# Agent attention into a squared-ReLU feed-forward: keys and values in tiles of 128 tokens, and the first batch in a fixed order

## The chip, the cores and the metric

The kernel runs on one core of a Trainium2 chip. The metric is the time of one execution on the device, in microseconds (us), lower is better. The core has five engines that matter here: PE (matrix products, with PEld for the loading of weights), DVE (vector), ACT (scalar functions), POOL (GpSimd) and SP, which issues all transfers. Each runs its own instructions in order and waits for the others by semaphores.

## The reference

Four batches of 12480 tokens with 128 channels, 49 agents per batch, all float32, and then one feed-forward layer over all 49920 tokens with 2048 hidden channels:

```python
def sm(a, b):
    s = scale * (a @ b.transpose(0, 2, 1))
    s = s - s.max(-1, keepdims=True)
    e = np.exp(s)
    return e / (e.sum(-1, keepdims=True) + 1e-09)
a2k = sm(agents, k)
agent_v = a2k @ v
q2a = sm(q, agents)
x = (q2a @ agent_v).reshape(B * S, D)
h = np.maximum(x @ w_in, 0.0)
return h * h @ w_out
```

The weights w_in and w_out come in as float64 and are read on the device as pairs of 32-bit words.

## The kernel before, in words

The attention output is never formed. For each batch the kernel makes a table: the 49 agents' value rows times w_in, 49 × 2048, scaled by the softmax denominators. A token's hidden row is then its 49 weights times that table. To keep float32 accuracy with the faster float32r products, numbers are split into a high and a low half: `aw_hi` holds the table's halves (98 rows, and 30 more rows of a cross term filled by a transfer), `aw_ex` the 19 remaining cross rows, repeated at four partition offsets.

**Stage A, keys of the first batch** (L443 to L446). Thirteen tiles of 960 keys are loaded (L141), each as 8 blocks of 120 tokens. `scores` (L150) multiplies each block with the agents on PE, ACT copies the result to `s` (L158), DVE keeps a running maximum `mx` (L163). `maxima` (L166) reduces it, transposes it on PE, and broadcasts the maximum of each agent to all partitions as `mb` (L183).

**Stage B, values of the first batch** (L452 to L465). Thirteen tiles of 960 values are loaded as 120 partitions × 8 × 128 (L147). `whole_values` (L192) subtracts `mb` on DVE, takes the exponential on ACT (L196), multiplies on PE with the exponentials as weights and the values as the moving side (L200), and adds the exponentials up in `es` on POOL (L206). `whole_sums` (L208) gathers both into `x`.

**Weights.** `decoded` (L90) turns 256 columns of float64 pairs into two float32 parts: one Abs on ACT (L98), five steps on DVE (L99 to L110). For w_in POOL adds the parts (L116). For w_out ACT casts the high half (L122) and POOL makes the low half in two steps (L123, L124). There are eight pieces of each. The w_in pieces are requested behind the keys and among the values; the w_out pieces are written last in the program (L472 to L477), the last four only behind the tables.

**Tables** (L243). Two small matmuls with `quad` fold the halves (L252, L253), four matmuls with w_in (L266) make the table, ACT and DVE write its halves (L268, L270), and SP moves the cross rows (L275, L277).

**Queries** (L282) make the weights of 960 tokens: scores (L290), softmax steps, the split (L190), two groups of four transposing matmuls (L312), an ACT copy into `w` (L317), and transfers of cross rows within `w` and into `x` (L320, L322).

**Main loop** (L482). Each step k handles 480 tokens by two chunks of 128 hidden channels. `first` (L341) makes the hidden rows `h` of two steps: four matmuls with `w`, four with `x`. `hidden` (L359) takes the relu `r` and the square's high half `g_hi` on ACT, the product `gg` on DVE, and the low half `g_lo` on POOL for even and on DVE for odd steps. `second` (L384), four steps later, adds six matmuls into `o`. Sixteen steps make a block of 960 tokens; 832 steps make the whole. The next batch's keys, values and tables (`background`, L401) and the next block's queries are put among these steps.

What sets the order: the main loop's instructions are chained one behind the other on each engine by `queued` (L334), the shown line of nearly all of them being L337. Everything else, all of the first batch too, is placed by a scheduler that goes by its own estimate of times, with `tc.high_priority()` at a few places; `step` (L421) holds the background behind the first batch's last instructions on three engines.

Of the kernel before, what the change touches and what calls it, by code (L numbers as in the profile page):

```python
# [38 lines left out]
def agent_attention_relu2(ctx: ExitStack, tc: tile.TileContext, qT, kT, v, agT, w_in, w_out, outT):  # L39
# [50 lines left out]
    def decoded(dec, src):  # L90

        raw = dec.tile([P, WCH, 2], U32, name="raw", bufs=4)
        flat = raw.rearrange("p n w -> p (n w)")
# [4 lines left out]
        nc.scalar.activation(t.bitcast(F32), high.bitcast(F32), AF.Abs)  # L98
        nc.vector.tensor_scalar(  # L99
# [3 lines left out]
        nc.vector.tensor_scalar(t, t, 0x07FFFFFF, 3, op0=ALU.bitwise_and, op1=ALU.logical_shift_left)  # L103
        nc.vector.scalar_tensor_tensor(
# [4 lines left out]
        nc.vector.tensor_single_scalar(rest.bitcast(U32), t, 0xFF800000, op=ALU.bitwise_and)  # L109
        nc.vector.scalar_tensor_tensor(out=rest, in0=low, scalar=2.0**-52, in1=rest, op0=ALU.mult, op1=ALU.mult)  # L110
        return t.bitcast(F32), rest

    def load_w_in(dec, n):
        cs = slice(n * WCH, (n + 1) * WCH)
# [1 line left out]
        nc.gpsimd.tensor_add(win[:, cs], t, rest)  # L116

    def load_w_out(dec, n):
        c = slice(n * WCH // C, (n + 1) * WCH // C)
        t, rest = decoded(dec, w_out.bitcast(U32).rearrange("(c p) d -> p c d", p=P)[:, c, :])  # L120
# [1 line left out]
        nc.scalar.copy(hi, t)  # L122
        nc.gpsimd.tensor_sub(t, t, hi.bitcast(F32))  # L123
        nc.gpsimd.tensor_add(lo, t, rest)  # L124
# [413 lines left out]
```

## Time and profile before

| | |
|---|---|
| median of 3 runs | 2059.88 us (2059.42 to 2061.74) |
| the profiled execution, its own time | 2060.99 us |
| its span from first to last instruction | 2059.2 us |
| PE busy | 2029.8 us, 99% |
| ACT, DVE, POOL busy | 1782.3, 1686.1, 1279.2 us |
| granted PE clock over the span | 0.992 |

Busy time is the union of an engine's instructions; a busy PE need not be at its peak. In a row of the timeline the first number is the start in us from the span's start, the second the duration. In a row of grouped instructions the last figures are the total busy time, the mean of one in ns, and the idle time of the engine just before them with what ended it. Shapes are partitions × elements. A window's row gives each engine's busy time with the number of instructions, then the granted clock (1.00 is full), the DMA engines' mean share and GB/s.

### The profile page before, as it was taken

What the parts mean: (1) busy time and instruction counts of PE and PEld (TensorE: products, weight loads), DVE (VectorE), ACT (ScalarE), POOL (GpSimd) and SP (SyncE); (2) the same over time, 40 slices, a digit from 0 to 9 for tenths busy, and PEclk for the clock granted to TensorE, in tenths of its full rate; (3) what the DMA queues carried; (4) which work ended last, traced back from release to release, by engine and by line L of the source; (5) the groups of instructions that cost most, each with busy time, mean ns of one, the idle gap of its engine ahead of it and who ended that gap; (6) DMA issues with size and microseconds to landing.
All of it is one profiled execution on the core that took longest, in us unless ns stands there. A gap on an engine that the chain in (4) does not pass through costs nothing.

```text
span 2059.2 us, 31857 instructions
## 1 busy us (share of the span) xinstructions
PE 2029.8 (99%) x11014; PEld 1589.8 (77%) x11014; DVE 1686.1 (82%) x1842; ACT 1782.3 (87%) x2100; POOL 1279.2 (62%) x1104
## 2 busy tenths in 40 slices
PE   9799999999999999999999999999999999999999
PEld 8588777777788777777778877777777777777777
DVE  5687888888887888888887788888888888888887
ACT  3478999989888899989888899998889898989897
POOL 3555787765544587776555467877555555656555
PEclk9799999999999999999999999999999999999999
DMA  9532122121122221221112212211111111111100
GB/s 288 160 92 76 59 72 74 53 77 41 45 81 65 62 72 54 72 71 57 55 54 69 68 42 61 74 58 49 42 50 36 45 36 46 37 41 36 38 23 20
DMA packets 55604, 131.36 MB, mean 64 GB/s; under 512 B 6660, under 2 KB 34388, under 8 KB 55444
## 3 DMA queue, kind: packets, MB, share of 16 engines
q1 hardware_dynamic: 55444, 129.33, 21.0%
q8 instruction: 88, 1.44, 0.3%
q14 instruction: 72, 0.59, 0.1%
HBM read 80.97 MB, written 25.56 MB: 52 GB/s over the span
## 4 chain that ended last, share of the span: by engine, by line
PE 53%; DVE 1%; issue 0%; ACT 0%
PE o L337 33%; PE h L337 16%; PE psa L290 2%; PE psa L155 1%; PE psa L312 1%; PE psa L235 1%; PE psa L266 0%; DVE h L337 0%; DVE gg L337 0%; DVE g_lo L337 0%; DVE z L301 0%; ACT r L337 0%; DVE ob L337 0%; ACT g_hi L337 0%; DVE av L241 0%
## 5 line engine op out<-in xcount | busy, mean ns | idle before, releaser
L372 POOL TENSOR_TENSOR g_lo<-gg,g_hi 128x480 fp32r<-128x480 f32 x832 | 999.2, 1222 | 685.7 <-DVE gg L337 489.1
L337 ACT ACTIVATE r<-h 128x960 f32<-128x960 f32 x832 | 800.9, 963 | 150.0 <-PE h L337 141.9
L337 ACT ACTIVATE g_hi<-r 128x960 fp32r<-128x960 f32 x832 | 837.7, 1007 | 34.1 <-POOL e L190 0.7
L337 DVE TENSOR_TENSOR h<-r,h 128x960 f32<-128x960 f32 x416 | 482.4, 1160 | 160.2 <-ACT r L337 157.8
L337 DVE TENSOR_TENSOR gg<-r,h 128x960 f32<-128x960 f32 x416 | 477.8, 1149 | 81.9 <-ACT r L337 81.0
L337 PE MATMUL o<-g_hi,wo_hi 128*128 128x480 f32 x1664 | 543.0, 408 | 0.0
L337 DVE TENSOR_TENSOR g_lo<-h,g_hi 128x960 fp32r<-128x960 f32 x416 | 480.8, 1156 | 45.2 <-ACT g_hi L337 8.1
L337 PE MATMUL o<-g_hi,wo_lo 128*128 128x480 f32 x1664 | 498.7, 381 | 0.0
L337 PE MATMUL o<-g_lo,wo_hi 128*128 128x480 f32 x1664 | 497.7, 380 | 0.0
L337 PE MATMUL h<-w,aw_hi 128*128 128x480 f32 x1664 | 483.3, 398 | 9.7 <-DVE gg L337 8.1
L337 PEld LDWEIGHTS o<-g_hi,wo_hi 128*128 128x128 f32 x1664 | 280.8, 188 | 118.8 <-issue 70.1
L337 PEld LDWEIGHTS o<-g_hi,wo_lo 128*128 128x128 f32 x1664 | 313.4, 188 | 51.3
L337 PEld LDWEIGHTS o<-g_lo,wo_hi 128*128 128x128 f32 x1664 | 313.0, 188 | 50.9
L337 PEld LDWEIGHTS h<-w,aw_hi 128*128 128x128 f32 x1664 | 289.0, 190 | 56.9 <-DVE gg L337 17.5
L337 PE MATMUL h<-x,aw_ex 19*128 19x480 f32 x1664 | 205.4, 481 | 0.1
L337 PEld LDWEIGHTS h<-x,aw_ex 19*128 19x128 f32 x1664 | 80.5, 182 | 140.7 <-issue 139.7
L290 PEld LDWEIGHTS psa<-ag,qt 128*120 128x120 f32 x816 | 102.2, 187 | 7.8 <-issue 1.4
L337 DVE COPY ob<-o 128x480 f32<-128x480 f32 x104 | 68.3, 656 | 39.8 <-PE o L337 38.3
L290 PE MATMUL psa<-ag,qt 128*120 128x49 f32 x816 | 98.1, 264 | 0.0
L190 POOL TENSOR_TENSOR vs<-vt,vs 120x1024 fp32r<-120x1024 f32 x39 | 86.3, 2213 | 16.7 <-ACT vs L188 16.4
L155 PEld LDWEIGHTS psa<-ag,kt 128*120 128x120 f32 x624 | 74.7, 185 | 4.8 <-DVE mx L163 0.6
L155 PE MATMUL psa<-ag,kt 128*120 128x49 f32 x624 | 71.9, 262 | 0.2 <-DVE mx L163 0.2
(109 smaller groups left out, 1026.6 us busy)
## 6 DMA issues: line engine op xcount, KB each, us to landing
qt<-in_qT SPq DMA_DIRECT2D x52, 480.0 KB
out_T<-ob SPq DMA_DIRECT2D x104, 240.0 KB
kt<-in_kT SPq DMA_DIRECT2D x39, 480.0 KB
vt<-in_v SPq DMA_DIRECT2D x39, 480.0 KB
x<-w SPq DMA_DIRECT2D x416, 35.6 KB
ahead<-in_kT SPq DMA_DIRECT2D x13, 480.0 KB
ahead<-in_v SPq DMA_DIRECT2D x13, 480.0 KB
w<-w SPq DMA_DIRECT2D x104, 56.2 KB
```

Source lines behind the costliest of these rows:

```text
L155: nc.tensor.matmul(sv[:, t, :], kt[:, t * TP : (t + 1) * TP], ag[:, b, :], start=True, stop=True)
L190: last[eng] = eng.tensor_sub(out[:, :, n : n + w], x, out[:, :, :w].bitcast(F32))
L235: nc.tensor.matmul(pv[:K2, :W], e[:, t, :], vs[:, t, :], start=(t == 0), stop=(t == NT - 1))
L290: nc.tensor.matmul(sv[:, t, :], qt[:, t * TP : (t + 1) * TP], ag[:, b, :], start=True, stop=True)
L312: nc.tensor.matmul(pt[:K2, t * TP : (t + 1) * TP], pp[:, j * (NT // 2) + t, :], identr, start=True, stop=True)
L337: ins = issue(*args, **kw)
L372: nc.gpsimd.tensor_sub(lo[:, n, :], gg[:, n, :], hi[:, n, :].bitcast(F32))
```

## The change

*Tiles.* The 12480 tokens of a batch are cut into 12 blocks of 8 × 128 tokens and a last one of 2 × 96, instead of 13 of 8 × 120. The host lays the keys out to match. Queries keep their 120.

*Order.* `queued` moves to the top, and wrappers `pe`, `act`, `dve`, `pool` and `sync` chain every instruction of the first batch behind the one written before it on its engine, so that this stage runs as written. It is written so: a w_in piece is requested behind each key tile and decoded between the scores; the query tile's scores lie between the transposition and the broadcast of the maxima; the w_out pieces are requested among the values; one is decoded in each of eight iterations of the values loop, ahead of the tables. The exponentials of a block are taken two iterations ahead, their subtraction in turn on POOL and DVE. `behind`, which holds the background, now names four engines.

*Products turned round.* `whole_values` takes the values as weights and the exponentials as moving side, so the result is already transposed; `quad` is not needed for the first batch, and the sum of exponentials is reduced twice into two halves.

```diff
+    blocks = [(i * KB, P, NT) for i in range(N // KB)] + [(N // KB * KB, N % KB // 2, 2)]
+    class Ordered:
+        def __getattr__(self, name):
+            issue = getattr(self.eng, name)
+            if not alone[0]:
+                return issue
+            return lambda *args, **kw: queued(issue, self.eng, *args, **kw)
+    pe, act, dve, pool, sync = (Ordered(e) for e in (nc.tensor, nc.scalar, nc.vector, nc.gpsimd, nc.sync))
...
-        vt = pool.tile([TP, NT, C], F32, name=name)
-        src = v[b, i * BLK : (i + 1) * BLK, :].rearrange("(p t) c -> p t c", p=TP)
-        last[nc.sync] = nc.sync.dma_start(vt, src)
+        at, rows, nt = blocks[i]
+        vt = pool.tile([P, KB], F32, name=name).rearrange("p (t c) -> p t c", c=C)
+        src = v[b, at : at + rows * nt, :].rearrange("(p t) c -> p t c", p=rows)
+        sync.dma_start(vt[:rows, :nt, :], src)
...
+    def whole_exps(b, i, eng):
+        _, rows, nt = blocks[i]
+        e = state[b]["s"][i][:rows, :nt, :]
+        less_maximum(b, i, e, eng)
+        act.activation(e, e, AF.Exp, scale=scale)
     def whole_values(b, i, vt):
-            nc.tensor.matmul(
-                st["pv"][:NA, :C], e[:, t, :], vt[:, t, :], start=(i == 0 and t == 0), stop=(i == NB - 1 and t == NT - 1)
+            pe.matmul(
+                st["pv"][:C, :NA], vt[:rows, t, :], e[:, t, :],
+                start=(i == 0 and t == 0), stop=(i == NK - 1 and t == nt - 1),
             )
...
-        for i in range(NB):
-            kt = load_keys(0, i, pre, "ahead")
-            run(scores(0, i, kt))
-        for n in range(WIN):
-            load_w_in(dec, n)
+        early = {i: i - 3 for i in range(3, 8)} | {9: 5, 11: 6}
+        for i in range(NK):
+            kts.append(load_keys(0, i, pre, "ahead"))
+            if 1 <= i <= NW:
+                raws[i - 1] = ask_w_in(dec, i - 1)
+            if i == NK - 3:
+                q0 = queries(0)
+                next(q0)
+            run(scores(0, i, kts[i]))
+            if i in early:
+                make_w_in(dec, early[i], raws.pop(early[i]))
+        top = maxima(0)
+        next(top)
+        next(top)
+        next(q0)
+        run(top)
+        for i in range(NK):
+            if i == NW:
+                make_w_in(dec, NW - 1, raws.pop(NW - 1))
+            vts.append(load_values(0, i, pre, "ahead"))
+            if 1 <= i <= NW:
+                raws[NW + i - 1] = ask_w_out(dec, i - 1)
+        for i in range(2):
+            whole_exps(0, i, (pool, dve)[i % 2])
+        for i in range(NK):
+            if i + 2 < NK:
+                whole_exps(0, i + 2, (pool, dve)[i % 2])
+            whole_values(0, i, vts[i])
+            next(q0, None)
+            if 3 <= i < NW + 3:
+                make_w_out(dec, i - 3, raws.pop(NW + i - 3))
         run(q0)
-    for n in range(NW):
-        with ExitStack() as es:
-            for ins in made if n >= EARLY else ():
-                es.enter_context(tc.issue_after(ins))
-            load_w_out(dec, n)
+        whole_sums(0)
+        run(tables(0))
+    behind = [chain[eng] for eng in (nc.sync, nc.scalar, nc.vector, nc.gpsimd)]
```

The built order shows three places. First ACT in the values stage, where `t<-raw` is the Abs that opens the decoding of a piece, `wo_hi<-t` its cast and `s<-s` the exponential of a block. Before:

```order
L196 ACTIVATE s_271<-s_271 120x392
L196 ACTIVATE s_285<-s_285 120x392
L98 ACTIVATE t_366<-raw_364 128x256
L196 ACTIVATE s_299<-s_299 120x392
L196 ACTIVATE s_313<-s_313 120x392
L188 CAST pp_530<-e_453 120x8x49
L98 ACTIVATE t_379<-raw_377 128x256
L98 ACTIVATE t_392<-raw_390 128x256
L98 ACTIVATE t_405<-raw_403 128x256
L317 CAST w0_560<-h_555 98x480
L98 ACTIVATE t_697<-raw_695 128x256
L98 ACTIVATE t_710<-raw_708 128x256
```

And in the change, in the middle of the values loop:

```order
L58 ACTIVATE s_293<-s_293 128x392
L58 CAST w0_573<-h_568 98x480
L58 ACTIVATE t_576<-raw_424 128x256
L58 CAST wo_hi_108<-t_576 128x256
L58 ACTIVATE s_318<-s_318 128x392
L58 ACTIVATE t_603<-raw_428 128x256
L58 CAST wo_hi_108<-t_603 128x256
L58 ACTIVATE s_332<-s_332 128x392
L58 CAST w1_630<-h_625 98x480
L58 ACTIVATE t_633<-raw_432 128x256
```

Before, exponentials came in a row and pieces were decoded two at a time behind them; now each exponential has one piece's Abs and cast behind it.

POOL in the same stage; `t<-t,wo_hi` and `wo_lo<-t,rest` finish a piece of w_out, `s<-s,mb` is a subtraction, and `mx` now holds the sum that `es` held. Before:

```order
L206 TENSOR_TENSOR es_478<-es_478,s_285 120x392
L116 TENSOR_TENSOR win_110<-t_405,rest_410 128x256
L206 TENSOR_TENSOR es_478<-es_478,s_299 120x392
L206 TENSOR_TENSOR es_478<-es_478,s_313 120x392
L123 TENSOR_TENSOR t_697<-t_697,wo_hi_111 128x256
L124 TENSOR_TENSOR wo_lo_112<-t_697,rest_702 128x256
```

In the change:

```order
L58 TENSOR_TENSOR t_576<-t_576,wo_hi_108 128x256
L58 TENSOR_TENSOR wo_lo_109<-t_576,rest_581 128x256
L58 TENSOR_TENSOR s_318<-s_318,mb_410 128x392
L58 TENSOR_TENSOR mx_146<-mx_146,s_268 128x392
L58 TENSOR_TENSOR t_603<-t_603,wo_hi_108 128x256
L58 TENSOR_TENSOR wo_lo_109<-t_603,rest_608 128x256
L58 TENSOR_TENSOR mx_146<-mx_146,s_293 128x392
```

The subtractions of every second block have moved to POOL, each behind the piece decoded before it, and the pieces of w_out stand ahead of the last sums.

PE at the first change of the token block, where `psa<-identr,pp` are the transposing matmuls of the second query tile and `h<-w` the first matmuls of two steps. Before, the w of the second tile (number 1016 there) is not yet used in these rows:

```order
L337 MATMUL h_1073<-w1_595,aw_hi_652 128x480 x2
L312 MATMUL psa_1011<-identr_94,pp_956 98x120 x4
L337 MATMUL h_1074<-w1_595,aw_hi_652 128x480 x2
L337 MATMUL h_1073<-x1_596,aw_ex_653 128x480 x2
L337 MATMUL h_1074<-x1_596,aw_ex_653 128x480 x2
L337 MATMUL o_920<-g_hi_972,wo_hi_111 128x480 x2
L337 MATMUL o_920<-g_hi_972,wo_lo_112 128x480 x2
L337 MATMUL o_920<-g_lo_974,wo_hi_111 128x480 x2
L337 MATMUL o_920<-g_hi_992,wo_hi_111 128x480 x2
L337 MATMUL o_920<-g_hi_992,wo_lo_112 128x480 x2
L337 MATMUL o_920<-g_lo_994,wo_hi_111 128x480 x2
L312 MATMUL psa_1065<-identr_94,pp_956 98x120 x4
```

In the change, where the w of the second tile is w0_999:

```order
L58 MATMUL o_1132<-g_lo_1095,wo_hi_108 128x480 x2
L183 MATMUL psa_985<-ag_82,kt_923 128x49 x8
L356 MATMUL psa_994<-identr_91,pp_939 98x120 x4
L356 MATMUL psa_1048<-identr_91,pp_939 98x120 x4
L58 MATMUL h_1209<-w0_999,aw_hi_738 128x480 x2
L58 MATMUL h_1210<-w0_999,aw_hi_738 128x480 x2
L183 MATMUL psa_1099<-ag_82,kt_983 128x49 x8
L58 MATMUL h_1209<-x0_1000,aw_ex_739 128x480 x2
L58 MATMUL h_1210<-x0_1000,aw_ex_739 128x480 x2
```

Both groups of transposing matmuls have moved to right ahead of the first matmul that uses their result. L58 in these rows is the line of `queued` in the changed kernel.

More of the change, by code (lines that the diff above doesn't have):

```diff
@@ L80, in agent_attention_relu2 @@
         )
-    split = [const.tile([TP, NT, 2 * (C + 1)], F32R, name=f"vs{i}") for i in range(2)]
+    split = [const.tile([P, NT, 2 * (C + 1)], F32R, name=f"vs{i}") for i in range(2)]
     for vs in split:
@@ L185, in halves, with less_maximum @@
+        dve.tensor_copy(st["mb"], pb[:, :NA])
     def halves(out, x, n, eng):
         w = x.shape[2]
-        nc.scalar.copy(out[:, :, :w], x)
+        act.copy(out[:, :, :w], x)
         yield
-        last[eng] = eng.tensor_sub(out[:, :, n : n + w], x, out[:, :, :w].bitcast(F32))
+        eng.tensor_sub(out[:, :, n : n + w], x, out[:, :, :w].bitcast(F32))
+    def less_maximum(b, i, out, eng):
+        st = state[b]
+        _, rows, nt = blocks[i]
+        mb = st["mb"][:rows, :].rearrange("p (o a) -> p o a", o=1).broadcast_to([rows, nt, NA])
+        eng.tensor_sub(out, st["s"][i][:rows, :nt, :], mb)
@@ L215, in whole_sums @@
-        pz = bank()
-        nc.tensor.matmul(pz[:NA, :1], e1, ones[:TP, :1], start=True, stop=True)
-        nc.vector.tensor_copy(x[:NA, C:], pz[:NA, :1])
-    def values(b, i, vt, eng):
+        e1 = small.tile([P, 2, NA], F32, name="e1")
+        for n in range(2):
+            dve.reduce_sum(e1[:, n, :], st["mx"].rearrange("p t a -> p a t"), axis=AX.X)
+        pz = bank()
+        pe.matmul(pz[:K2, :1], e1.rearrange("p h a -> p (h a)"), ones[:, :1], start=True, stop=True)
+        rl = st["rl"] = small.tile([K2, 1], F32, name="rl")
@@ L220, in values @@
+        dve.tensor_scalar_add(rl, pz[:K2, :1], 1e-9)
+        dve.reciprocal(rl, rl)
+        av = st["avT"] = small.tile([C, K2], F32, name="avT")
+        act.copy(av[:, :NA], st["pv"][:C, :NA])
+        dve.tensor_copy(av[:, NA:], st["pv"][:C, :NA])
+    def values(b, i, vt):
         st = state[b]
-        s = st["s"][i]
-        mb = st["mb"].rearrange("p (o a) -> p o a", o=1).broadcast_to([TP, NT, NA])
-        d = small.tile([TP, NT, NA], F32, name="d", bufs=2)
-        eng.tensor_sub(d, s, mb)
+        _, rows, nt = blocks[i]
+        d = small.tile([P, NT, NA], F32, name="d", bufs=2)[:rows, :nt, :]
+        less_maximum(b, i, d, pool)
@@ L232, in values @@
         yield
         pv = bank()
-        for t in range(NT):
-            nc.tensor.matmul(pv[:K2, :W], e[:, t, :], vs[:, t, :], start=(t == 0), stop=(t == NT - 1))
+        for t in range(nt):
+            pe.matmul(pv[:K2, :W], e[:, t, :], vs[:rows, t, :], start=(t == 0), stop=(t == nt - 1))
         yield
@@ L450, in agent_attention_relu2 @@
         next(q0)
[L451 to L452 removed]
+        run(top)
+        for i in range(NK):
+            if i == NW:
+                make_w_in(dec, NW - 1, raws.pop(NW - 1))
             vts.append(load_values(0, i, pre, "ahead"))
[L454 to L460 removed]
+            if 1 <= i <= NW:
+                raws[NW + i - 1] = ask_w_out(dec, i - 1)
```

258 lines of the change are left out of this document (121 added, 137 removed).

## The prediction

> **What bounds the kernel now.** I read the page first, then the busy time by windows, then the timeline of the first 140 us for the anchors, and the groups of instructions for durations.
>
> ```profile
> 8.00:20.00 12.00, 12.00 (x117) 12.00 (x117) 3.94 (x7) 3.40 (x7) 0.00 (x0) 1.00 1.03 407
> 35.10:64.90 29.80, 21.54 (x171) 20.77 (x172) 19.28 (x34) 8.47 (x18) 17.85 (x18) 0.84 1.00 247
> 83.70:105.00 21.30, 17.70 (x71) 12.71 (x71) 19.60 (x27) 15.77 (x23) 13.21 (x11) 0.68 0.42 108
> 160.00:2059.20 1899.20, 1890.16 (x10110) 1470.53 (x10108) 1574.69 (x1661) 1698.34 (x1973) 1206.80 (x1021) 1.00 0.18 54
> ```
>
> The columns of a window are its length, the busy time of PE, PEld, DVE, ACT and POOL, the clock, the DMA share and GB/s. From 160 us on PE is busy for 1890 of 1899 us at full clock: the main loop is bound by PE, and only less PE work or an earlier start moves the end. Before that lie two weak stretches: the values stage (35 to 65 us, loads at 247 GB/s, share 1.00) and the first 21 us of the main loop (clock 0.68). So the question is when PE gets a steady main loop. The anchors are these:
>
> ```profile
> 72.78 1.88 PE L155 MATMUL psa<-ag,kt 128*120 128x49 f32 x16
> ...
> 77.44 5.11 PE L266 MATMUL h<-win,avT 128*98 128x512 f32 x8 [0.76 <-ACT avT L256]
> ...
> 83.68 0.74 PEld L337 LDWEIGHTS h<-w,aw_hi 128*128 128x128 f32 x4 [1.98 <-DVE aw_lo L270]
> ```
>
> The second batch's first scores run at 72.8, the table of the first batch starts at 77.4, the main loop at 83.7.
>
> **The change, part by part.** *Keys.* Keys, query tile and the eight w_in pieces now interleave: 9.0 MB, of which all but the first 0.5 MB come after the first score at 407 GB/s, 21 us, so the last tile is scored near 29.7, against 28.7 now. Behind it DVE has a decode (2 us), a maximum and a reduction, so the transposition of the maxima comes near 33.4. Then the query tile's scores stand on PE between it and the broadcast:
>
> ```profile
> 28.54 1.84 PE L290 MATMUL h<-ag,qt 128*120 128x49 f32 x16
> ...
> 30.43 0.80 DVE L169 TENSOR_REDUCE m<-mx 120x49 f32<-120x392 f32 x1
> ...
> 93.83 3.44 PE L290 MATMUL psa<-ag,qt 128*120 128x49 f32 x16
> ```
>
> They cost 1.84 us at full and 3.44 at half clock; PE has just idled 3.7 us, so I take the latter. With 0.9 for the broadcast and its copy, mb is ready at 37.7 (36.1 to 38).
>
> *Values stage: a chain instead of a load.* One iteration that decodes a piece of w_out I call a round; there are eight. The reader finds the order of ACT and POOL in the section on the change. In it ACT takes a piece's Abs only after the exponential of the block two ahead, which waits for that block's subtraction, on POOL in one iteration and on DVE in the next, itself behind the preceding round's decoding. Behind that exponential on ACT stand Abs and the cast, and for them wait DVE's five steps and POOL's two.
>
> ```profile
> L224 POOL TENSOR_TENSOR d<-s,mb 120x392 f32<-120x392 f32 x39 | 37.2, 961 | 0.0
> ...
> L196 ACT ACTIVATE s<-s 120x392 f32<-120x392 f32 x13 | 6.5, 528 | 5.5 <-DVE s L195 5.5
> ...
> L98 ACT ACTIVATE t<-raw 128x256 f32<-128x256 f32 x16 | 6.7, 434 | 23.1 <-DMA raw<-in_w_out 10.8 <-DMA raw<-in_w_in 7.3 <-POOL es L206 2.5
> ...
> L99 DVE TENSOR_SCALAR t<-t 128x256 f32<-128x256 f32 x16 | 10.0, 628 | 10.7 <-ACT t L98 9.9 <-POOL win L116 0.9
> ...
> L103 DVE TENSOR_SCALAR t<-t 128x256 uint32<-128x256 uint32 x16 | 5.5, 351 | 0.2
> ...
> L104 DVE SCALAR_TENSOR_TENSOR t<-raw,t 128x256 uint32<-128x256 uint32 x16 | 7.5, 476 | 0.1
> ...
> L109 DVE TENSOR_SCALAR rest<-t 128x256 uint32<-128x256 uint32 x16 | 6.5, 403 | 0.3
> ...
> L110 DVE SCALAR_TENSOR_TENSOR rest<-raw,rest 128x256 f32<-128x256 uint32 x16 | 9.9, 617 | 0.2
> ...
> L195 DVE TENSOR_TENSOR s<-s,mb 120x392 f32<-120x392 f32 x13 | 9.6, 808 | 0.0
> ...
> L122 ACT CAST wo_hi<-t 128x256 fp32r<-128x256 f32 x8 | 3.2, 405 | 7.4 <-DVE t L104 7.4
> ...
> L123 POOL TENSOR_TENSOR t<-t,wo_hi 128x256 f32<-128x256 f32 x8 | 6.9, 862 | 10.3 <-ACT wo_hi L122 10.0 <-DVE rest L109 0.3
> ...
> L124 POOL TENSOR_TENSOR wo_lo<-t,rest 128x256 fp32r<-128x256 f32 x8 | 6.1, 764 | 0.7 <-DVE rest L110 0.4
> ...
> L206 POOL TENSOR_TENSOR es<-es,s 120x392 f32<-120x392 f32 x11 | 12.1, 1097 | 0.5
> ```
>
> A POOL round runs 0.96 (subtraction) + 0.53 + 0.43 + 1.46 (three DVE steps) + 1.02 (two more) = 4.40; the DVE round behind it 0.81 + 0.53 + 0.43 + 1.46 + 0.41 + 0.86 + 0.76 = 5.26. With some ten handovers of 0.04 a pair takes 9.7 to 10.1; I take 4.9 a round, 39.2 in all. These means contain waits of DVE for POOL:
>
> ```profile
> 48.27 0.95 POOL L190 TENSOR_TENSOR pp<-e,pp 120x392 fp32r<-120x392 f32 x1 [1.83 <-ACT pp L188]
> ...
> 48.42 1.08 DVE L110 SCALAR_TENSOR_TENSOR rest<-raw,rest 128x256 f32<-128x256 uint32 x1
> ...
> 52.58 0.42 DVE L110 SCALAR_TENSOR_TENSOR rest<-raw,rest 128x256 f32<-128x256 uint32 x1
> ```
>
> The same step took 1.08 us beside a POOL instruction and 0.42 alone. So 0.42 of L110's mean 0.617 is its own work. With every DVE step at that share, 0.68, of its mean, the pair loses 0.32 × (2 × 1.46 + 1.02 + 0.81) = 1.5: a round of 4.2, 33.6 in all, is the lower bound. [...]
>
> Ahead of the first round, after mb: the last w_in decode (2.0), then on POOL its addition (0.76), three subtractions and the query product (0.96 each) and two sums (1.10), then a cast (0.5): 9.3, with handovers 9.7. Behind the last: two sums (1.1 and a short 0.3), now two reductions of 0.8, one matmul and the small steps to the table (1.1): 4.1. Turning the products round and dropping the matmuls with quad lies on PE, which in this stage waits for the exponentials; if that cover went, 13 blocks of 16 passes of 0.115 would be 24 us, still less than the rounds.
>
> The table thus starts at 37.7 + 9.7 + 39.2 + 4.1 = 90.7 instead of 77.4: **+13.3** (+7 to +15).
>
> Where the loads go: with 128 partitions I expect 400 GB/s, so values and w_out (8.5 MB) are there near 50; at 247 they would be near 64. The last block is used near 83, so neither counts; if the chain were not there, the loads would cost up to 14. On SP the requests for w_out move ahead of the second batch's first keys and values, and those go behind the tables' copies. The batch's first scores stand behind the first o's in PE's order, so their landing may cost one 1.8 us wait, which the range below holds.
>
> *Start of the main loop.* The instruction counts of 83.6 to 105 and a clean stretch:
>
> ```profile
> L337 PE MATMUL h<-w,aw_hi 128*128 128x480 f32 x12 | 5.2, 545 | 4.7 <-DVE gg L337 3.2 <-DVE aw_lo L270 1.2 <-PE psa L290 0.3
> ...
> L337 PE MATMUL o<-g_hi,wo_hi 128*128 128x480 f32 x4 | 2.2, 643 | 0.0
> ...
> L155 PE MATMUL psa<-ag,kt 128*120 128x49 f32 x19 | 2.3, 267 | 0.0
> ...
> 1600.77 1.04 PE L337 MATMUL h<-w,aw_hi 128*128 128x480 f32 x4
> ...
> 1602.17 0.70 PE L337 MATMUL o<-g_hi,wo_hi 128*128 128x480 f32 x2
> ...
> 1604.89 1.04 PE L337 MATMUL h<-w,aw_hi 128*128 128x480 f32 x4
> ```
>
> Cleanly, four h with their x take 1.40 us, twelve o 2.72. So these 21.3 us did 3 × 1.40 + 2.72 + 35 score passes of 0.115 (1.84 / 16) = 10.9, lost 10.4, and had 1.9 in hand (72.78): net 8.5. Part of that is DVE decoding w_out there, which the change takes away. What stays is the filling of the pipeline:
>
> ```profile
> L337 ACT ACTIVATE r<-h 128x960 f32<-128x960 f32 x832 | 800.9, 963 | 150.0 <-PE h L337 141.9
> ...
> L337 ACT ACTIVATE g_hi<-r 128x960 fp32r<-128x960 f32 x832 | 837.7, 1007 | 34.1 <-POOL e L190 0.7
> ```
>
> The third pair of h waits for buffers that four ACT steps (3.94) and a DVE step free, so the first o comes about 9 us after the first h with 4.2 us of work done; 1 more for a clock near 0.5: 6 lost. **−2.5** (−4.5 to 0).
>
> *First change of the token block.* The built order puts both transpositions of the second query tile right ahead of the first matmul that needs them; now they stand 14.5 us ahead:
>
> ```profile
> 69.38 0.84 SPq L320 DMA_DIRECT2D w<-w  x1
> ...
> 70.27 2.88 SPq L322 DMA_DIRECT2D x<-w  x4
> ...
> 80.99 0.86 SPq L275 DMA_DIRECT2D aw_hi<-aw_lo  x1
> ...
> 117.32 0.48 PE L312 MATMUL psa<-identr,pp 120*98 120x120 f32 x4
> ...
> 131.87 0.60 PE L337 MATMUL h<-w,aw_hi 128*128 128x480 f32 x2
> ```
>
> A cast (as L196, 0.5) behind a relu or square in ACT's queue (1.0, the row of r above), issues of 0.84 + 2.88, and a landing of 1.8 (81.85 to 83.68) make 7.0 us. Behind the waiting matmul stand the next scores, 1.8, and with the first h, 0.9, that is all that PE can do meanwhile. With 1 for the wait ahead of the transpositions, for POOL's half of pp: **+5** (+2 to +8).
>
> *Batches 2 to 4.* Six of 104 value matmuls a batch go:
>
> ```profile
> L235 PE MATMUL psa<-vs,e 120*98 120x258 f32 x312 | 43.8, 283 | 0.0
> ```
>
> 18 × 43.8 / 312 = **−2.5**. Score passes become fewer (36 in three batches) but their weights wider, 128 columns for 120. No row has that form, so the saving lies between 0, if a pass grows with its columns, and 36 × 0.115 = 4 if it does not; I take 0, since the weights' bytes stay the same, and keep the 4 in the range. The reordered keys and the removed quad cost no measured time.
>
> Sum: 13.3 − 2.5 + 5 − 2.5 = +13.3 on the profiled execution's 2060.99, 2074.3; its time is 1.1 above the median, so 2073.
>
> **The rivals.** *Load-bound* (faster): the values stage is set by its loads, now and after. For it: share 1.00 at 247 GB/s. 7.4 MB at 407 would take 18.1 instead of 29.8. It decides if a round takes under its block's load, 0.8 MB or 2 us. Then −11.7 − 2.5 − 2.5 + 5: 2048. Against it: no chain of the rows above gets under 4.2. [...]
>
> *POOL's pace* (near 2060): ACT and DVE run far enough ahead that only POOL's work counts, 0.48 + 1.10 + 1.63 = 3.2 a round. −13.6 from the sum: 2059, or 2056 with a block change at 2.
>
> *Unblocked:* rounds of 4.2, block change at 2: 2073 − 5.6 − 3 = 2064.
>
> *Worse:* half clock until 115 and a block change of 8: 2080.
>
> **How the numbers follow.** Forecast 2073: 0.60. Load-bound 0.08, POOL's pace 0.12, unblocked 0.10, worse 0.10. The range 2058 to 2084 leaves out load-bound and half of POOL's pace. About 0.2%, 4 us, is what a measurement can tell. Faster: 0.08 + half of 0.12 = 0.14; same: 0.06 and a fifth of unblocked, 0.08; slower 0.78.
>
> **What would show it.** Right: table matmul near 91, wo_hi casts 4 to 5 us apart, loads over near 50 at about 400 GB/s, a PE gap of 5 us at the first block change, full PE from there. Wrong: casts 2 to 3 us apart, a table before 78, or no gap.

## The result: 28 us slower, and the profile after

The kernel after takes 2089.24 us (median of 4 runs, 2088.95 to 2089.47), the kernel before 2060.79 (4 runs, 2059.42 to 2061.74): a ratio of 1.0138, 95% interval 1.0121 to 1.0156. The profiled execution took 2089.47 us with a span of 2087.6, against 2060.99 and 2059.2. The forecast of 2073 had the direction and less than half of the size (12 us of 28); 2089 lies outside its range of 2058 to 2084.

The first view is the busy time by windows (columns as before: length, busy time of PE, PEld, DVE, ACT, POOL, clock, DMA share, GB/s). A window's count of instructions includes those under way at its edges.

```profile
4.09:7.50 3.41, 3.41 (x33) 3.41 (x32) 0.00 (x0) 0.00 (x0) 0.00 (x0) 1.00 0.98 360
7.50:10.91 3.41, 3.41 (x33) 3.41 (x32) 1.12 (x2) 0.97 (x2) 0.00 (x0) 1.00 1.00 370
10.91:14.33 3.42, 3.42 (x19) 3.42 (x17) 0.57 (x2) 0.48 (x1) 0.00 (x0) 0.50 1.03 405
35.10:64.90 29.80, 21.77 (x104) 21.39 (x103) 14.46 (x36) 7.21 (x17) 11.15 (x13) 0.50 0.46 163
...
83.70:105.00 21.30, 15.98 (x73) 15.34 (x72) 10.69 (x26) 5.75 (x15) 13.84 (x17) 0.50 0.04 13
160.00:2087.00 1927.00, 1913.00 (x10255) 1498.51 (x10255) 1593.24 (x1686) 1713.51 (x2000) 1210.70 (x1032) 1.00 0.18 55
```

The clock column is the news. PE's clock falls to half at 10.9 us and comes back at 113.3 (and is at half once more from 120.1 to 127.0). It falls while PE is busy for all of every window (3.41 of 3.41 us in the two ahead of 10.9): no pause of PE stands ahead of it. In the kernel before the clock was full in the scores and in most of the values stage; a stretch of its scores, then a step of its values stage at half clock and the one behind it:

```profile
12.10:15.51 3.41, 3.41 (x35) 3.41 (x34) 1.12 (x2) 1.02 (x3) 0.00 (x0) 1.00 1.03 406
36.00:39.41 3.41, 3.41 (x18) 3.33 (x17) 3.41 (x3) 1.59 (x4) 3.25 (x3) 0.50 0.98 252
39.41:42.83 3.42, 3.42 (x34) 3.42 (x33) 3.42 (x5) 1.34 (x3) 2.53 (x3) 1.00 0.99 243
```

The timeline of the kernel after:

```profile
35.77 7.67 PE L58 MATMUL h<-ag,ahead 128*128 128x49 f32 x36
...
51.03 0.21 DVE L58 COPY mb<-h 128x49 f32<-128x49 f32 x1 [3.14 <-PE h L58]
...
68.47 0.40 ACT L58 CAST wo_hi<-t 128x256 fp32r<-128x256 f32 x1 [1.97 <-DVE t L58]
...
77.03 0.56 ACT L58 CAST w<-h 98x480 fp32r<-98x480 f32 x1 [6.23 <-PE h L58]
...
79.14 0.41 ACT L58 CAST wo_hi<-t 128x256 fp32r<-128x256 f32 x1 [1.22 <-DVE t L58]
...
108.76 5.92 PE L58 MATMUL h<-win,avT 128*98 128x512 f32 x8 [0.56 <-DVE avT L58]
```

Each float32 matmul of a block appears as two passes on PE, 16 for a block of eight. At half clock a score pass takes 0.213 us (7.67 / 36), so the last keys are scored near 43 instead of 29.7, and mb comes at 51.2 instead of 37.7. The eight casts of wo_hi come at 62.6, 68.5, 79.1, 84.3, 88.6, 93.8, 98.0 and 102.5. Six of the seven gaps average 4.9; one is 10.7. In that one ACT waits 6.23 us for PE: the query tile's transposition stands in PE's order behind value products that run at half speed, and in ACT's order its cast stands ahead of the next piece's magnitude. The first table matmul comes at 108.76 instead of 77.44.

The first change of the token block, in the timeline:

```profile
126.93 0.43 SPq L329 DMA_DIRECT2D qt<-in_qT  x1
...
146.61 1.78 PE L334 MATMUL psa<-ag,qt 128*120 128x49 f32 x16
...
161.21 0.89 PE L356 MATMUL psa<-identr,pp 120*98 120x120 f32 x4 [1.51 <-DVE mx L192]
...
162.75 0.92 PE L356 MATMUL psa<-identr,pp 120*98 120x120 f32 x4 [0.65 <-ACT w L361]
...
165.00 1.97 PE L58 MATMUL h<-w,aw_hi 128*128 128x480 f32 x4 [1.34 <-DMA w<-w]
...
172.10 0.76 PE L58 MATMUL h<-x,aw_ex 19*128 19x480 f32 x1 [0.77 <-DMA x<-w]
172.79 0.50 PEld L58 LDWEIGHTS o<-g_hi,wo_hi 128*128 128x128 f32 x2 [0.41 <-issue]
```

The second query tile is asked for at 126.9, behind the copies of the tables. The transpositions come at 161.2, the matmuls that need them wait for the copies of w and x, and the clock is at half again from 161.1 to 178.2. All that PE waited for between 144 and 182 us (total, times, longest):

```profile
PE psa L356 <- DVE mx L192: 1.5, 1, 1.5
PE h L58 <- DMA w<-w: 1.3, 1, 1.3
PE h L58 <- DMA x<-w: 0.8, 1, 0.8
PE psa L356 <- ACT w L361: 0.6, 1, 0.6
```

To see what each stretch costs, I count the o matmuls in the trace (six to a step) and compare when a step's first one begins:

| step | before | after | difference |
|---|---|---|---|
| (first table matmul) | 77.4 | 108.8 | +31.3 |
| 0 | 100.4 | 124.9 | +24.6 |
| 10 | 129.1 | 155.1 | +26.0 |
| 18 | 152.3 | 192.8 | +40.4 |
| 208 | 610.2 | 649.7 | +39.5 |
| 416 | 1112.0 | 1148.2 | +36.2 |
| 624 | 1606.3 | 1638.6 | +32.4 |
| 831 | 2053.7 | 2081.9 | +28.2 |

So: +31.3 up to the table, −5.3 in the main loop's start, +14.4 at the block change, and −12.2 over the rest: 0.9 up to step 208, then 3.3, 3.8 and 4.2 a batch, the last batch included, in which no other batch's attention runs. The forecast had +13.3, −2.5, +5 and −2.5.

### The profile page after: what moved, and what is told of

It is laid out like the page before. It is cut to its first block, busy times and chain, and to the rows that moved or that the text cites. A ratio compares the mean times of both kernels' runs of the same rounds, so it can differ in the third digit from the quotient of the medians.

```text
span 2087.6 us, 31676 instructions
## 1 busy us (share of the span) xinstructions
PE 2051.5 (98%) x10932; PEld 1621.5 (78%) x10932; DVE 1672.7 (80%) x1835; ACT 1775.2 (85%) x2100; POOL 1275.1 (61%) x1110
## 5 line engine op out<-in xcount | busy, mean ns | idle before, releaser
L58 ACT ACTIVATE r<-h 128x960 f32<-128x960 f32 x832 | 800.7, 962 | 145.5 <-PE h L58 132.7
L58 ACT ACTIVATE g_hi<-r 128x960 fp32r<-128x960 f32 x832 | 837.5, 1007 | 34.8 <-PE o L58 1.0
L58 DVE TENSOR_TENSOR h<-r,h 128x960 f32<-128x960 f32 x416 | 482.5, 1160 | 156.7 <-ACT r L58 151.6
L58 DVE TENSOR_TENSOR gg<-r,h 128x960 f32<-128x960 f32 x416 | 478.0, 1149 | 85.4 <-ACT r L58 79.9
L58 PE MATMUL o<-g_hi,wo_hi 128*128 128x480 f32 x1664 | 539.2, 405 | 0.0
L58 DVE TENSOR_TENSOR g_lo<-h,g_hi 128x960 fp32r<-128x960 f32 x416 | 481.0, 1156 | 48.3 <-ACT g_hi L58 7.7
L58 PE MATMUL h<-w,aw_hi 128*128 128x480 f32 x1664 | 485.4, 398 | 10.7 <-DVE gg L58 7.7
L58 PE MATMUL o<-g_hi,wo_lo 128*128 128x480 f32 x1664 | 495.4, 379 | 0.0
L58 PE MATMUL o<-g_lo,wo_hi 128*128 128x480 f32 x1664 | 494.7, 378 | 0.0
L58 PEld LDWEIGHTS o<-g_hi,wo_hi 128*128 128x128 f32 x1664 | 280.9, 188 | 117.4 <-issue 69.5
L58 PEld LDWEIGHTS o<-g_hi,wo_lo 128*128 128x128 f32 x1664 | 313.3, 188 | 47.2
L58 PEld LDWEIGHTS o<-g_lo,wo_hi 128*128 128x128 f32 x1664 | 313.3, 188 | 46.7
L58 PEld LDWEIGHTS h<-w,aw_hi 128*128 128x128 f32 x1664 | 289.3, 190 | 59.3 <-DVE gg L58 20.3
L58 PE MATMUL h<-x,aw_ex 19*128 19x480 f32 x1664 | 207.9, 481 | 1.3 <-DMA x<-w 1.0
L58 PEld LDWEIGHTS h<-x,aw_ex 19*128 19x128 f32 x1664 | 81.6, 182 | 142.4 <-issue 138.1
L58 DVE COPY ob<-o 128x480 f32<-128x480 f32 x104 | 68.2, 656 | 35.9 <-PE o L58 35.5
L219 POOL TENSOR_TENSOR vs<-vt,vs 128x1024 fp32r<-128x1024 f32 (+1 forms) x39 | 81.6, 2094 | 12.6 <-ACT vs L217 12.3
L183 PEld LDWEIGHTS psa<-ag,kt 128*128 128x128 f32 (+1 forms) x588 | 76.4, 195 | 3.6
L183 PE MATMUL psa<-ag,kt 128*128 128x49 f32 (+1 forms) x588 | 72.7, 271 | 0.0
```

Source lines behind the costliest of these rows:

```text
L58: ins = issue(*args, **kw)
L183: pe.matmul(sv[:, t, :], kt[:, t * rows : (t + 1) * rows], ag[:, b, :], start=True, stop=True)
L219: eng.tensor_sub(out[:, :, n : n + w], x, out[:, :, :w].bitcast(F32))
```

## Experiments: the clock

Theory: the granted clock follows how many columns PE streams, not whether it is busy. A pass takes 0.11 us at full clock behind 128 × 128 weights whether it streams 49 columns or 128 (the kernel after, up to 10.9 us: 0.112 in the median from one begin to the next, for 43 passes of 49 and for 31 of 128). Rival: the fixed order sets the pace, and the clock only follows it. Behind each time stands its ratio to the kernel before, measured beside it, with a 95% interval. `...` marks lines left out.

**64 columns.** Edit, in scores and in products alike:

```diff
-            pe.matmul(sv[:, t, :], kt[:, t * rows : (t + 1) * rows], ag[:, b, :], start=True, stop=True)
+            pe.matmul(sw[:, t, :], kt[:, t * rows : (t + 1) * rows], cols, start=True, stop=True)
...
```

> The kernel after, but the first batch's scores and value products stream 64 columns in each pass instead of 49 (the 15 more are neighbours' columns and their results are not read); PE's passes there take 0.111 us at full clock whether they stream 49 or 128 columns, so the work costs no more. Clock theory (PE's clock is granted by how much of PE's time goes into streaming columns; 49 columns behind weights of 128 x 128 are too few to hold it or to get it back): the clock stays at 1.00 from 4 us through the scores, mb is ready near 37 instead of 51, the long round of 10.7 us is gone, the first table matmul comes near 91 instead of 108.8, and the time is 2070 to 2074. Order theory (the interleaved loads and the fixed order set the pace and the clock only follows): 2087 to 2091 and half clock as now.

Measured: 2075.63, ratio 1.0082 (1.0065 to 1.0099). The windows of a score step and of a product step:

```profile
13.80:17.20 3.40, 3.40 (x33) 3.40 (x32) 2.07 (x6) 1.44 (x4) 0.00 (x0) 1.00 1.05 405
...
47.90:51.30 3.40, 3.40 (x18) 3.40 (x17) 1.73 (x5) 1.60 (x4) 1.79 (x3) 0.50 0.44 154
```

Fifteen unused columns a pass hold the clock through the scores (full until 30.9), and mb comes at 39.2. But in PE's pause around mb the clock falls, and 64 columns do not get it back: the 10.7 us round stays, the table comes at 96.7. Half of the theory's forecast, then. At half clock 16 passes begin in 3.41 us, 994 columns here; at full clock, from 13.8 to 17.2, it was 31 passes, 1984 columns.

**Products turned back**, exponentials as weights, values streamed (128 columns):

```diff
-                st["pv"][:C, :NA], vt[:rows, t, :], e[:, t, :],
+                st["pv"][:NA, :C], e[:, t, :], vt[:rows, t, :],
...
```

> The kernel after, but the first batch's value products are turned back: exponentials as weights (49 columns wide), values streamed, 128 columns a pass, with the matmuls by quad at the end. Clock theory: half clock through the scores as now (mb at 51), but granted in full a few us after the products begin, near 60 to 63, so that the query tile's transposition no longer waits behind half-speed products: the 10.7 us round falls to 5, the table comes near 102, time 2081 to 2084. Order theory: no change, 2088 to 2092.

```profile
56.70:60.10 3.40, 3.40 (x18) 3.23 (x17) 2.04 (x4) 1.75 (x5) 2.99 (x4) 0.50 0.36 145
60.10:63.50 3.40, 3.40 (x33) 3.40 (x32) 1.74 (x5) 1.47 (x4) 1.78 (x3) 1.00 0.60 183
```

The clock returns behind the first window filled with 128-column passes, the casts are 4.8 apart, and the table comes at 102.1, all as forecast. Yet the time was 2092.32, ratio 1.0157 (1.0142 to 1.0172): the main loop had become slower. That is taken up below.

**Tiles of 120 tokens** in the kernel after, order and turn kept:

```diff
-KB = P * NT
+KB = BLK
...
-    blocks = [(i * KB, P, NT) for i in range(N // KB)] + [(N // KB * KB, N % KB // 2, 2)]
+    blocks = [(i * KB, TP, NT) for i in range(N // KB)]
...
```

> The kernel after, but keys and values in tiles of 120 tokens again (13 blocks of 960), order and turned products kept. Clock theory: full clock through the scores, since a pass of 49 columns behind 120-wide weights takes 0.105 and held the clock in the kernel before; mb near 38. The products (49 columns, weights of 120 x 128) then start behind a pause of PE: if the clock is not granted again, 208 passes of 0.213 make 44 us and the table comes near 98, time 2080 to 2084 with the 18 value matmuls of batches 2 to 4 back; if it is, 2074 to 2077. The values' loads should fall to about 250 GB/s and last until 65. Order theory: clock falls near 11 us as now, 2090 to 2094.

```profile
11.25:14.70 3.45, 3.41 (x32) 3.28 (x31) 1.45 (x4) 1.30 (x3) 0.00 (x0) 1.00 1.04 410
14.70:18.10 3.40, 3.40 (x19) 3.40 (x18) 3.19 (x9) 0.82 (x2) 0.72 (x1) 0.50 1.03 398
```

Measured: 2085.53, ratio 1.0125 (1.011 to 1.014). The clock fell here too, at 14.7, which the theory had not forecast. In the 3.41 us ahead of that only 30 passes began, where the kernel before had 32 or 33: the pieces of w_in between the keys (0.26 MB to each 0.49 MB, at 400 GB/s 1.9 us a tile against 1.67 of passes) make PE wait; two passes begin 0.21 and 0.31 us behind the one before, where the others take 0.105. So the wider weights (31 passes in the kernel after, with no such gap) and the interleaved loads each bring the number of passes in a step under that of the kernel before. The time lies outside the ranges of both theories. With the table at 106.4, 120 tokens take 2.0 us more from step 18 to step 831 than the kernel after (1891.2 and 1889.1).

**The turn alone**, in the kernel before:

```diff
-                st["pv"][:NA, :C], e[:, t, :], vt[:, t, :], start=(i == 0 and t == 0), stop=(i == NB - 1 and t == NT - 1)
+                st["pv"][:C, :NA], vt[:, t, :], e[:, t, :], start=(i == 0 and t == 0), stop=(i == NB - 1 and t == NT - 1)
...
```

> The kernel before with the first batch's value products turned round and the matmuls by quad dropped for it, nothing else changed. Clock theory: the clock falls in PE's pause ahead of the products (32.6) as before, but is not granted again at 39.4; the products run at 0.213 us a pass, 44 us from 35, so that they end near 80 to 82 instead of 72, the table comes near 86 instead of 77.4, and the time is 2066 to 2071. Order theory: the turn does nothing but save the matmuls by quad, 2058 to 2061.

```profile
35.20:65.90 30.70, 30.70 (x147) 30.70 (x146) 22.67 (x34) 7.80 (x18) 17.91 (x18) 0.50 0.99 252
...
90.09 5.22 PE L269 MATMUL h<-win,avT 128*98 128x512 f32 x8
```

Measured: 2073.24, ratio 1.0064 (1.0049 to 1.0079). PE is busy for all of 30.7 us at half clock; the table comes at 90.1 instead of 77.4. One swap of operands, with fewer matmuls behind it, costs 13 us. The order theory's 2058 to 2061 is out; the clock theory had the course right (0.50 in this window, 0.84 in the kernel before from 35.1 to 64.9) and 2 to 7 us too little (2066 to 2071, table near 86).

**128 columns** in scores and turned products of the kernel after:

```diff
+        w = 128 if alone[0] else NA
...
+        cols = ag.rearrange("c b a -> c (b a)")[:, b * NA : b * NA + w]
...
+            w = min(128, (nt - t) * NA)
...
```

> The kernel after, but the first batch's scores and turned products stream 128 columns in each pass instead of 49 (79 of them neighbours' columns whose results are not read; the last two or three passes of a block's products stream fewer). Clock theory: full clock through the scores as with 64 columns, and now granted again within two of its 3.4 us steps after the products begin, so that the round of 10.7 us goes too: mb near 39, casts of wo_hi 4.8 apart, table near 90, time 2067 to 2071. Weight theory (weights of 128 x 128 keep the clock down whatever is streamed behind them): as with 64 columns, 2074 to 2077.

```profile
36.79 0.21 DVE L58 COPY mb<-h 128x49 f32<-128x49 f32 x1 [2.15 <-PE h L58]
...
58.55 0.41 ACT L58 CAST wo_hi<-t 128x256 fp32r<-128x256 f32 x1 [1.22 <-DVE t L58]
63.70 0.41 ACT L58 CAST wo_hi<-t 128x256 fp32r<-128x256 f32 x1 [1.22 <-DVE t L58]
...
88.18 6.13 PE L58 MATMUL h<-win,avT 128*98 128x512 f32 x8 [0.56 <-DVE avT L58]
```

Measured: 2070.94, ratio 1.0051 (1.0036 to 1.0067), as the clock theory said; the weight theory is out. With its clock the values stage is what the prediction had summed up: mb at 37.0, rounds of 4.8, table at 88.2. The clock falls here too in PE's pause around mb, and comes back behind the first step filled with such passes:

```profile
41.95:45.36 3.41, 3.41 (x18) 3.41 (x18) 1.89 (x4) 1.90 (x4) 3.00 (x5) 0.50 1.04 395
45.36:48.80 3.44, 3.44 (x32) 3.44 (x32) 1.61 (x6) 1.79 (x4) 1.83 (x2) 1.00 0.73 267
```

## Experiments: the late query tile

```diff
+        asked = chain[nc.sync]
         run(tables(0))
-    behind = [chain[eng] for eng in (nc.sync, nc.scalar, nc.vector, nc.gpsimd)]
+    behind = [asked] + [chain[eng] for eng in (nc.scalar, nc.vector, nc.gpsimd)]
```

> The kernel after, but the second batch's loads (first keys, first values, next query tile) may be asked for right behind the first batch's loads instead of behind the copies of the tables; PE's order at the first change of the token block then has the transpositions some 8 steps earlier. Load theory (the stall of some 15 us between the tenth and the fourteenth step comes from the query tile that arrives too late): first o within 3 us of 125, but the loss at the block change falls under 3 us, time 2073 to 2079. Chain theory (the steps from the query scores to the transposed weights are too long whenever they start): 2087 to 2091.

```profile
91.95 0.43 SPq L329 DMA_DIRECT2D qt<-in_qT  x1
...
123.41 3.44 PE L334 MATMUL psa<-ag,qt 128*120 128x49 f32 x16
...
145.76 0.48 PE L356 MATMUL psa<-identr,pp 120*98 120x120 f32 x4
```

Measured: 2075.04, ratio 1.0065 (1.0047 to 1.0083). The tile is asked for 35 us earlier, and the transpositions stand 15 us earlier than they did. Steps 10 and 14 begin 11.7 us apart instead of 26.0, and the clock stays full through the change (its mean over the span is 0.972, against 0.969 in the kernel after). The first o came at 129.2, 4.3 us later than in the kernel after, which the load theory had not forecast (within 3). The chain theory is out: no wait of PE is left at the change, though 22 us lie between the tile's scores and its transpositions, against 14.6 in the kernel after. No engine of the kernel after waits for the query tile itself; its scores stand late in PE's order, at 146.6, and the edit moves them in the built order as well as the load. So what cost the 14 us is the tile's late request together with the late place of its steps; the two were not separated.

## Experiments: the pitch of the main loop

Two clean steps take 4.12 us in the kernel before (shown in the prediction) and 4.08 after:

```profile
1619.24 1.04 PE L58 MATMUL h<-w,aw_hi 128*128 128x480 f32 x4
...
1623.32 1.02 PE L58 MATMUL h<-w,aw_hi 128*128 128x480 f32 x4
```

The instructions are the same. In the kernel with the products turned back they take 4.13 again (h at 1653.17 and 1657.30). What differs there is only the size of small tiles ahead of the main loop's: everything behind lies 192 bytes a partition lower in SBUF. So I moved it back, and moved the kernel before's tiles up by 160 (a tile of 40):

```diff
+    small.tile([P, 48], F32, name="gap")
     aw = ctx.enter_context(tc.tile_pool(name="aw", bufs=2))
```

> The kernel of e2_unturned with an unused tile of 192 bytes a partition ahead of the main loop's tiles, so that the tables, the query tiles and everything of the main loop lie at the same places in SBUF as in the kernel after (in e2_unturned they lay 192 bytes lower). Address theory (where these tiles lie sets the pitch of the main loop's passes): a step of the last batch falls from 2.156 us to 2.137 as in the kernel after, and the time from 2092.3 to 2080 to 2082, the first o staying near 118.7. Work theory (the slower steps of e2_unturned come from what it does or from the chip, not from addresses): 2091 to 2094.

> The kernel before with an unused tile of 160 bytes a partition ahead of the main loop's tiles, nothing else. Address theory, with a pattern that repeats within 1024 bytes (the tables and main loop tiles then lie as in the kernel after, modulo 1024): a step of the last batch falls from 2.157 to 2.137 us, and the time to 2044 to 2050. Address theory with a longer pattern: anything between 2044 and 2062. Work theory: 2058 to 2062.

The two kernels' h of successive pairs of steps:

```profile
1644.96 1.04 PE L58 MATMUL h<-w,aw_hi 128*128 128x480 f32 x4
1649.03 1.03 PE L58 MATMUL h<-w,aw_hi 128*128 128x480 f32 x4
```

```profile
1615.59 1.04 PE L338 MATMUL h<-w,aw_hi 128*128 128x480 f32 x4
1619.66 1.04 PE L338 MATMUL h<-w,aw_hi 128*128 128x480 f32 x4
```

Both take 4.07. The first measured 2081.53, ratio 1.0102 (1.0087 to 1.0117), 10.8 less than without its gap. The second measured 2048.74, ratio 0.9943 (0.9927 to 0.9958): an unused tile of 160 bytes makes the kernel before 12.9 us faster. From step 18 to step 831 the kernel before took 1901.4 us, with the unused tile 1888.9, and the kernel after 1889.1: the tile alone accounts for the whole −12.2 of the table above. The kernel after has the better pitch though nothing in the diff aims at it. Why these addresses are better, and of which tile, was not tried.

## Experiments: the decoding, and both repairs

**Both repairs** (128 columns, loads first):

> The kernel after with both repairs, 128 columns a pass (e6_wide128) and the second batch's loads ahead of the tables' copies (e7_loads_first), the decoding left in the values stage. If the two costs are separate they add up: 2089.2 - 18.3 - 14.2 = 2056.7, 2054 to 2060. If a faster start brings another wait ahead of the first block change, 2062 or more.

The edits are the two shown above. Measured: 2053.03, ratio 0.9955 (0.994 to 0.9969), 1 us under the forecast range: together the repairs give 36.2 us, 3.7 more than the two apart (18.3 and 14.2), and the repaired change is faster than the kernel before. It is not faster than the kernel before with the gap, whose interval overlaps its own.

**Decoding moved behind the table.** The first two tries also cut the buffers of encoded pieces to four, and that held up other loads:

```diff
-            if 3 <= i < NW + 3:
-                make_w_out(dec, i - 3, raws.pop(NW + i - 3))
...
+            make_w_out(dec, n, raws.pop(NW + n) if NW + n in raws else ask_w_out(dec, n))
```

> The kernel of e6_wide128 (128 columns a pass in scores and turned products), with the decoding of w_out taken out of the values stage: the first four pieces may be decoded at any time, the last four behind the table's steps, in the scheduler's order as in the kernel before. Chain theory (eight rounds of 4.8 us, the decoding's chain, set the values stage): without them a block costs what POOL (0.95 every second block and 1.0 for the sum) or PE (1.8) needs, 13 blocks near 24 us from 41; the first table matmul comes near 68 to 72 instead of 88. The decoding then lies beside the first steps of the main loop and costs there 6 to 10 of the 18 gained: 2059 to 2065. Load theory (the values come no faster than the rounds): table at 85 or later, 2070 or more.

> The kernel of e9_decode_behind, with the second batch's loads allowed ahead of the tables' copies as in e7_loads_first. If the three costs (clock, rounds, late query tile) are separate, this takes another 12 to 14 us off e9_decode_behind: 2046 to 2052, faster than the kernel before and about the same as the kernel before with the gap. If the decoding in the main loop's start and the earlier loads collide, 2055 or more.

Measured: 2063.03, ratio 1.0008 (0.9998 to 1.0017), and 2063.71, ratio 1.0012 (1.0003 to 1.0021). In both, keys waited behind w_in's pieces for a buffer (mb at 47.8 and 45.9), in the second PE also stood 6.84 us for the second batch's keys ahead of the table. Neither answers the question. The third try gave the late pieces buffers of their own, and again fewer to the rest (9 instead of 11 for keys and values, 6 instead of 8 for encoded pieces). Its control, with the decoding left in the rounds, has only the first edit:

```diff
-    behind = [asked] + [chain[eng] for eng in (nc.scalar, nc.vector, nc.gpsimd)]
+    behind = [asked] + [chain[eng] for eng in (nc.tensor, nc.scalar, nc.vector, nc.gpsimd)]
...
+    late = ctx.enter_context(tc.tile_pool(name="late", bufs=2))
...
+            make_w_out(late, n, w_outs[n] if n < 4 else ask_w_out(late, n))
...
```

> The kernel of e14_scores_late (both repairs, the second batch's first scores behind the table's matmuls on PE) with the whole decoding of w_out behind the table's steps, its first four pieces in buffers of their own, so that neither the keys nor the second batch's loads wait for a buffer of it as they did in e9_decode_behind and e10_behind_loads. Chain theory (the decoding is what makes the values stage 39 us long, and DVE and POOL have room for it later): mb near 37, products over by 64 to 68, table 68 to 74, time 2038 to 2044. Give-back theory (in the main loop's start the decoding costs what it cost between the products, since DVE and POOL are wanted there too): table as early, but the fourth step's o no earlier than in e14_scores_late, 2049 to 2054.

> The kernel of e11_wide_loads, with the second batch's first scores held behind the table's matmuls on PE, since in e12_halves_apart PE stood 5.5 us for their keys in the middle of the products. If that wait lay on the path: 2 to 4 us less than e11_wide_loads, 2049 to 2051; if it was covered by the rounds: 2052 to 2054. Control for e13_decode_late.

The timeline and two windows of the third try:

```profile
69.02 3.76 PE L58 MATMUL h<-win,avT 128*98 128x512 f32 x8 [0.56 <-DVE avT L58]
80.54 1.94 PE L58 MATMUL h<-w,aw_hi 128*128 128x480 f32 x4 [1.60 <-DMA aw_hi<-aw_lo]
```

```profile
44.00:64.00 20.00, 20.00 (x167) 20.00 (x168) 5.70 (x7) 7.11 (x16) 18.17 (x19) 0.91 0.29 94
80.54:115.70 35.16, 31.65 (x134) 23.78 (x135) 33.26 (x57) 24.01 (x37) 25.26 (x24) 0.65 0.43 142
```

Measured: 2051.70, ratio 0.9958 (0.9943 to 0.9972); the control 2053.09, ratio 0.9968 (0.9955 to 0.9981). The table comes 19 us earlier than the control's 88.0, the first o 8 us earlier, step 8 begins 1 us later, step 18 is 2.5 us ahead. In the values stage PE is then the limit: it is busy for all of the 20 us, in one stretch up to the sums, with POOL close behind (18.2 of 20). In the main loop's start DVE is busy for 33.3 of 35.2 us and PE's clock is 0.65. The time is that of the give-back theory; its sign came later than it said, since the fourth step's o was still 6.4 us earlier (113.5 against 119.9) and the gain was gone by step 8. So moving the decoding behind the table won nothing that can be measured (1.4 us, overlapping intervals); what the fewer buffers cost in it was not separated. The control beside both repairs (2053.09 and 2053.03) shows that PE's wait for the second batch's keys was covered.

**Rounds without the chain**: each piece's cast and POOL steps one iteration later, on top of both repairs.

```diff
+            if half:
+                make_w_out(i - 4, *half.pop())
             if 3 <= i < NW + 3:
-                make_w_out(dec, i - 3, raws.pop(NW + i - 3))
+                half.append(decoded(dec, raws.pop(NW + i - 3)))
...
```

> The kernel of e11_wide_loads, with each piece of w_out decoded in two halves: the magnitude and DVE's five steps in one iteration of the values loop, ACT's cast and POOL's two steps in the next, so that no engine waits there for the one before it; the same instructions otherwise. Chain theory (a round of 4.8 us is the chain exponential, magnitude, three DVE steps, cast, POOL; by POOL's own work it would be 0.5 + 1.0 + 0.9 + 0.7 = 3.1): casts of wo_hi 3.1 to 3.8 apart, the first table matmul 8 to 13 us earlier than 88.2, time 2041 to 2046. Work theory (the engines are as busy as DVE and POOL beside each other allow): casts 4.5 or more apart, 2050 to 2054.

Measured: 2051.93, ratio 0.9959 (0.9945 to 0.9972), casts 4.5 apart and the table at 87.3: a miss for the chain theory, and no clear gain over both repairs (2053.03). PE waited 5.49 us for the second batch's keys at 76.8 here, but afterwards still 2.47 us for the sums ahead of the table. Four rounds here, and four rounds with the chain (128 columns):

```profile
56.17:74.92 18.75, 9.77 (x69) 9.22 (x68) 15.28 (x22) 5.12 (x14) 12.42 (x14) 0.91 0.28 89
```

```profile
54.22:73.18 18.96, 11.38 (x83) 10.83 (x82) 8.95 (x23) 5.97 (x15) 12.43 (x14) 0.90 0.07 20
```

The same work of DVE is busy for 15.28 instead of 8.95 us: freed of the chain, its steps take longer (the second step with raw, `t<-raw,t`, 1.137 us instead of 0.426 on average), and DVE and POOL are busy side by side for at least 8.95 of the 18.75 us (15.28 + 12.42), with the chain for at least 2.42 of 18.96 (8.95 + 12.43). That the two beside each other set the 4.5 is the author's estimate from these sums, not tested.

## Why the prediction was too low, point by point

Two terms failed. The scores and products were summed at PE's full clock, and the table came 31.3 us later instead of 13.3; and the block change held the wait but not the half clock behind it, 14.4 us instead of 5.

- *mb at 37.7*: 51.2. The step that failed is "the last tile is scored near 29.7". It took the scores' pace from the loads and left PE's clock at full, though the change made the weights wider and put w_in's loads between the keys. With the clock held, mb came at 37.0, 14.2 us earlier.
- *Lead-in 9.7*: from mb at 51.2 to the first magnitude at 60.9, 9.7.
- *Rounds of 4.9*: 4.9 but for the one that waits for PE, 4.8 with the clock repaired. The size was right. The reason was right in that steps of DVE take longer beside POOL's (1.08 us against 0.42 in the rows of the prediction); how much of a round that makes was not separated. It was wrong in the chain: taken apart, the chain gave 0.3 a round.
- *Turning the products is covered; "if that cover went, 13 blocks of 16 passes of 0.115 would be 24 us, still less than the rounds"*: this is the other half of the failure. The 24 us were worked out at full clock. The turned products did not bring the clock back (0.50 up to 113.3 us), took 0.213 a pass, and a transposition queued among them held ACT for 6 us.
- *Table +13.3*: +31.3; +10.7 with the clock repaired. The term was sized well for the kernel it described.
- *Start of the main loop −2.5*: −5.3 from the table to step 10, somewhat beyond the −4.5 given as the bound. *Block change +5 (+2 to +8)*: +14.4. The place and the sign were right, and so nearly was the wait: PE's waits there add to 4.2. What the sum left out is the clock, at half for 17.1 us behind that wait; an estimate of its cost is 7 us, half of the 14 or so in which PE was busy meanwhile. The remaining 3 are not accounted for.
- *Batches 2 to 4, −2.5*: the tiles gave 2.0 (against the kernel with 120 tokens); the score passes saved nothing, as taken (0.111 against 0.105 a pass). But the main loop gained 12.2 in all, as much as the kernel before gains from the unused tile alone (12.5): a term that the sum did not have. It was luck for the forecast, which without it would have been some 10 us further off.
- *Loads at 400 GB/s with 128 partitions*: 395 GB/s in a window of the kernel with 128 columns while values flow (41.95 to 45.36), against 233 with 120 partitions in the fixed order (40 to 55). Their end near 50 was wrong (65, since they wait for buffers), and cost nothing.
- *Rivals*: the nearest was the one called worse, half clock until 115 and a block change of 8, 2080 at a chance of 0.10. The clock was at half until 113, and the block change cost 14.4. Both together were priced at 7 us with no working shown; on the scores and products alone the clock cost 18 us (2089.2 to 2070.9).

The balance: the clock in scores and products 18.3, the late query tile 14.2 (2089.2 to 2075.0), both together 36.2, and against them 12 from addresses. What is left of the change, repaired and at the same pitch, is no gain: 2053.0 beside 2048.7, 4.3 more, with overlapping intervals.

## What to carry to other kernels

When a change alters the shape of PE's passes, sum PE's time at both clocks (here 0.111 and 0.213 us a pass) before calling it covered: here 79 unused columns a pass, at the same 0.11 us, kept full clock through the scores, and streaming the 128 columns of the values instead of 49 brought it back at 60.1 instead of 113.3 us. Before moving work off a stage, ask which engine does it and whether that engine has room in the next one; here moving the decoding won nothing clear. And compare the pitch of untouched loops in both traces: a shift of addresses (here 160 bytes, 12.9 us) can hide a loss, or pass for a gain.

## What the runs showed of the hardware

In the traces of the kernels before and after, every change of the clock lies a multiple of 3.41 us behind the one before (30, 2, 2, 10 and 5 times in the kernel after). Six such steps of the first batch, by the passes that begin in them:

| run, from (us) | passes | columns | clock in the step | clock behind it |
|---|---|---|---|---|
| before, 12.1 | 32 of 49 | 1568 | 1.00 | 1.00 |
| after, 7.5 | 31 of 49 | 1519 | 1.00 | 0.50 |
| tiles of 120, 11.25 | 30 of 49 | 1470 | 1.00 | 0.50 |
| before, 36.0 | 16 of 128 | 2048 | 0.50 | 1.00 |
| after, 10.9 | 16 of 49 | 784 | 0.50 | 0.50 |
| 64 columns, 44.5 | 16 of 64 or 49 | 994 | 0.50 | 0.50 |

These are single steps, and what decides between them was not shown. The count of columns alone does not: in the kernel before, half clock stayed behind nine passes of 480 in the step from 97.4 us (PE busy for 3.30 of 3.41) and ended behind nine in the next (3.41 of 3.41). The surprise is that no pause of PE stands ahead of the longest stretch: in the kernel after, half clock lasted 102 us (10.9 to 113.3), begun behind two steps in which PE was busy for 3.41 of 3.41 us.

The second surprise is the address: 160 or 192 bytes a partition moved the pitch of the same passes by 1% (4.12 or 4.13 to 4.07 us for two steps), 11 to 13 us over this kernel.
